# A DiT block on one core: first K block and last x tile loaded by columns, image 0's last K tile spread over the scale bank, other PSUM banks for image 1

## The chip, the cores and the metric

The kernel runs on one core of a Trainium2 chip. The metric is the device time of one execution in microseconds (us); shorter is better. A core has TensorE (PE, the matmuls; PEld are its weight loads), VectorE (DVE), ScalarE (ACT), GpSimd (POOL), SyncE (SP, which issues most loads), an on-chip memory of 128 partitions, and PSUM, eight banks of 512 fp32 columns in which matmuls leave their results and from which DVE and ACT read them.

## The reference

One transformer block with adaptive layer norm: x is 2 images of 256 tokens with D = 1152, in bf16.

```
mod = (silu(c) @ w_mod).reshape(B, 6, 1, D)
shift_a, scale_a, gate_a, shift_m, scale_m, gate_m = [mod[:, i] for i in range(6)]
h = layernorm(x) * (1 + scale_a) + shift_a
q, k, v = split(h @ wqkv), two heads of 576
a = softmax(q k^T * 576**-0.5) v, heads joined, @ wo
x = x + gate_a * a
h2 = layernorm(x) * (1 + scale_m) + shift_m
return x + gate_m * (gelu(h2 @ w_fc1) @ w_fc2)
```

The change lies in the first part: from the loads to the end of k. The shift is left out of k (it adds the same to every score of a query), so k needs only the scaled layer norm, which the kernel calls HK; q and v use HX, which is HK plus the shift.

## The kernel before, in words

D is cut into nine blocks of 128 rows (kt = 0 to 8), the same nine for the contraction and for the output features (f or j = 0 to 8). A token tile t is 128 tokens; tiles 0 and 1 are image 0, tiles 2 and 3 image 1. All loads of the start stand in one SP queue in the order written: x tiles 0 to 2, the scale part of w_mod for kt 0 to 4 (WSC, in four loads), K blocks 0 and 1 (WK), x tile 3, K blocks 2 to 4, WSC for the rest, K blocks 5 to 8, the shift part (WSH), then the Q blocks (WQ, over WSC's place).

PE goes through the start in the order of the program text. Scale matmuls (sca) sum up the scales of blocks 0 to 4 in bank 7, the very first in bank 3. The normalised x (XN) is transposed by tile: xn_T(t) writes nine transposes into the places that xt_ps(b, kt) names. From there hk(kt, b) makes HK = transposed x times scale. For kt 0 to 4 (KC = 5) hk reads PSUM itself (L832 on DVE, L830 on ACT); the others are copied first (xn_T_copy, L688) and scaled once their scales are known. k_pair(kts, i, b) multiplies the K columns of features 2i and 2i+1 with HK of image b, both halves in one bank, KB[b][i]. Image 0 has four pairs in banks 0 to 3. Image 1 has three pairs. What is left over is feature 6 and 7 of image 1 and feature 8 of both images; feature 8 is one projection of 512 columns at the end of the K phase (proj(WK, 8, 17, HK, 7)).

In the middle stands scb: 36 small matmuls that sum up the scales of blocks 5 to 8 in the first 128 columns of bank 7. DVE transposes them in two steps (scb_T5 and scb_T6, L907), adds one (L909), and makes hk_5 to hk_8 from them. After the K pairs come the shift matmuls (sh, bank 0), their transpose on DVE (L952), and HX (L961 on DVE, L958 on ACT). Then q: for each kt six matmuls of 512 columns into six banks:

```
qb = (2, 3, 4, 5, 6, 1)
for kt in range(KT):
    for j in range(KG):
        mm(ps32(qb[j]), WQ[:, kt, j * 128:(j + 1) * 128], HX[:, kt, :], kt == 0, kt == KT - 1)
```

A small planner orders the work and inserts the waits. PE and SP keep the order of the text. ACT and DVE begin with lists written by hand (S.first): DVE has hk_0_1, hk_2_1, hk_4_1, scb_T5, sc1a_5, hk_5_0, hk_5_1, scb_T6, sc1a_6 near the end of its list, ACT ends with xn_2, hk_4_0, hk_1_1, hk_3_1, xnT_cp1_5 (the second number is the image). After its list an engine takes, of what is ready by the planner's own durations, the operation with the longest remaining path. Waits come from what each instruction reads and writes. In PSUM the planner keeps books by whole bank:

```
if eng == "pe":
    if self.bank_other[b]:
        self.bank_prev_other[b] = self.bank_other[b]
        self.bank_other[b] = []
        self.bank_pe[b] = []
    for o in self.bank_prev_other[b]:
        self._add_dep(ins, o)
...
else:
    for u in self.bank_pe[b]:
        self._add_dep(ins, u.instrs[-1])
    for o in self.bank_other[b]:
        if o.unit.eng != eng:
            self._add_dep(ins, o)
```

That is: a matmul that writes a bank waits for all operations of ACT and DVE that read the bank earlier in the text; an operation of ACT or DVE waits for the last matmul of each PE unit in the bank, and for all earlier operations of the other of the two engines in that bank.

Behind the K phase and q follow scores and softmax, v, the output projection, the second layer norm and the MLP; the change doesn't touch them.

Of the kernel before, what the change touches and what calls it, by code (L numbers as in the profile page):

```python
# [497 lines left out]
P = 128  # L498
NTOK = 512
D = 1152  # L500
KT = 9
# [5 lines left out]
CH = 384  # L507
NCH = 3
F0 = 9
KC = 5  # L510
# [5 lines left out]
def c_mm(n):  # L516
    return max(n / 2.4 + 2.5, 27.0)


def c_act(n, aps=0):  # L520
    return 190.0 + 0.8 * n + 75.0 * aps


def c_dve_psum32(n):
    return 110.0 + 1.13 * n


def c_dve_psum16(n):
    return 110.0 + 0.57 * n
# [14 lines left out]
def build_kernel(nc, x, c, wqkv, wo, w_mod, w_fc1, w_fc2, out):  # L544
    S = Sched()
# [4 lines left out]
    with (  # L550
# [4 lines left out]
        def sb(off, nbytes, dt=BF16):  # L555
            assert off % 4 == 0 and off + nbytes <= ARENA_BYTES, (off, nbytes)
            v = arena[:, off // 2:(off + nbytes) // 2]
            if dt == F32:
                v = v.bitcast(F32)
            return v  # L560

        def ps32(bank, c0=0, n=512):
            return psum[:, bank * 512 + c0: bank * 512 + c0 + n]

        def ps16(bank, c0=0, n=1024):
            v = psum[:, bank * 512: (bank + 1) * 512].bitcast(BF16)
            return v[:, c0:c0 + n]
# [21 lines left out]
        def wmat(o, f):  # L589
            return sb(o, KT * f * 2).rearrange("p (k f) -> p k f", k=KT)  # L590
# [3 lines left out]
        WK = wmat(O_B, D)  # L594
# [10 lines left out]
        X = sb(O_X, 9216).rearrange("p (t d) -> p t d", t=4)  # L605
        XN = sb(O_QK, 9216).rearrange("p (t d) -> p t d", t=4)
        HX = sb(O_HX, 9216).rearrange("p (k t) -> p k t", k=KT)
        HK = sb(O_HK, 9216).rearrange("p (k t) -> p k t", k=KT)
        QK = sb(O_QK, 18432).rearrange("p (j t) -> p j t", j=18)
# [54 lines left out]
        xv = x.rearrange("b (p t) d -> b p t d", t=2)  # L664
        outv = out.rearrange("b (p t) d -> b p t d", t=2)
        wqkv_v = wqkv.rearrange("(k p) f -> p k f", p=P)
# [5 lines left out]
        def dma(dst, src, nbytes, name, is_out=False, eng="sp", run=4096):  # L672
            eff = 1.0 if run >= 4096 else (1.08 if run >= 2304 else (1.15 if run >= 1536 else (1.3 if run >= 1024 else 1.42)))
            return S.op(eng, 500.0 if eng == "sp" else 150.0, lambda e: e.dma_start(dst, src), reads=[src], writes=[dst],  # L674
                        name=name, dma_bytes=nbytes * eff, is_out=is_out)

        def dve(cost, fn, reads, writes, name):
            return S.op("dve", cost, fn, reads=reads, writes=writes, name=name)

        def act(cost, fn, reads, writes, name):  # L680
            return S.op("act", cost, fn, reads=reads, writes=writes, name=name)
# [4 lines left out]
        def copy_on(eng, dst, src, n, psum16, name):  # L686
            if eng == "act":
                act(c_act(n), lambda e: e.activation(out=dst, in_=src, func=ACTF.Copy), [src], [dst], name)  # L688
            else:
                dve(c_dve_psum16(n) if psum16 else c_dve_psum32(n), lambda e: e.tensor_copy(dst, src), [src], [dst], name)  # L690

        def mm(o, l, r, st, sp, **kw):
            S.instr(lambda e: e.matmul(o, lhsT=l, rhs=r, start=st, stop=sp, **kw), reads=[l, r], writes=[o])  # L693

        def tr(o, i_, idn):
            S.instr(lambda e: e.transpose(o, i_, idn), reads=[i_, idn], writes=[o])  # L696
# [6 lines left out]
        for (ka, kb, cuts) in ((0, KC, (0, 2, 5, 8, 9)), (KC, KT, (0, 3, 6, 9))):  # L703
            w = (kb - ka) * P
            for k0, k1 in zip(cuts, cuts[1:]):
                dma(WSC[:, k0:k1, ka * P:kb * P], wmod_v[:, k0:k1, D + ka * P:D + kb * P], (k1 - k0) * P * w * 2,
                    "ld_sc%d_%d" % (ka, k0), run=w * 2)
            for kt in range(ka, kb):
                dma(WK[:, kt, :], wqkv_v[:, kt, D:2 * D], P * D * 2, "ld_wk%d" % kt, run=2304)
                if kt == 1:  # L710
                    dma(X[:, 3, :], xv[1][:, 1, :], P * D * 2, "ld_x3", run=2304)
        for k0 in range(0, KT, 3):
            dma(WSH[:, k0:k0 + 3, :], wmod_v[:, k0:k0 + 3, 0:D], 3 * P * D * 2, "ld_sh%d" % k0, run=2304)

# [61 lines left out]

        def xt_ps(b, kt, n=1):
            if b == 0:
                return (4, 5, 6)[kt // 4], (kt % 4) * 256
            return (7, (kt - KC) * 256) if kt >= KC else ((6, 4)[kt % 2], kt // 2 * 256)  # L780

        def xn_T(t, part="", kts=range(KT)):
            b = t // 2
            S.unit("pe", len(kts) * c_mm(128), "xnT_%d%s" % (t, part))
            for kt in kts:
                bank, c0 = xt_ps(b, kt)
                tr(ps16(bank, c0 + (t % 2) * 128, 128), XN[:, t, kt * 128:(kt + 1) * 128], IDENT)
# [47 lines left out]
        def k_mm(kts, j, b, bank, half):  # L835

            for kt in kts:
                mm(ps32(bank, half * 256, 256), WK[:, kt, j * 128:(j + 1) * 128], HK[:, kt, b * 256:(b + 1) * 256], kt == 0 and half == 0,
                   kt == KT - 1, skip_group_check=True)

        KB = [(0, 1, 2, 3), (5, 6, 4)]
        ev_rr = [0]

        def k_pair(kts, i, b, bank=None):
            S.unit("pe", 2 * len(kts) * c_mm(256), "k%d_%d_%d" % (b, i, kts[0]))
            bank = KB[b][i] if bank is None else bank
            if kts[0] == 0:
                for kt in kts:
                    for half in range(2):
                        k_mm((kt,), 2 * i + half, b, bank, half)  # L850
            else:
                for half in range(2):
                    k_mm(kts, 2 * i + half, b, bank, half)
            if kts[-1] == KT - 1:
                eng = "act" if ev_rr[0] % 2 == 0 else "dve"
                ev_rr[0] += 1
                copy_on(eng, QK[:, 9 + 2 * i:11 + 2 * i, b * 256:(b + 1) * 256], ps32(bank).rearrange("p (j t) -> p j t", j=2), 512, False,
                        "k_ev%d_%d" % (b, i))
# [25 lines left out]
        for kt in range(KC):  # L884
            for i in range(2 if kt == KC - 1 else 4):
                k_pair((kt,), i, 0)
            if kt == 1:
                xn_T(2)
        xn_T(3, "a", range(KC))
        k_pair((KC - 1,), 2, 0)  # L890
        xn_T(3, "b", range(KC, KT))
# [3 lines left out]
            hk(kt, 1, "act" if kt % 2 else "dve")  # L895
        k_pair((0, 2, 1, 4, 3), 0, 1)
        k_pair((0, 2, 1), 1, 1)
        S.unit("pe", KC * c_mm(256), "k1_6_0")
        for i, kt in enumerate((0, 2, 1, 4, 3)):
            mm(ps32(7, 256, 256), WK[:, kt, 768:896], HK[:, kt, 256:512], i == 0, False, skip_group_check=True)  # L900
        S.unit("pe", KT * 4 * 27.0, "scb")
        for kt in range(KT):
            quad_mm(7, WSC[:, kt, :], KC, KT, kt, False)
# [8 lines left out]
                hk(kt, b)  # L912
        k_pair((4, 3), 1, 1)
        k_pair((0, 2, 1, 4, 3), 2, 1)
        for kt in range(KT):
            dma(WQ[:, kt, :], wqkv_v[:, kt, 0:D], P * D * 2, "ld_wq%d" % kt, run=2304)
        for kt in range(KC, KT - 2):
# [7 lines left out]
        def qk_evac(j, bank):  # L925
            copy_on("act" if ev_rr[0] % 2 == 0 else "dve", QK[:, j, :], ps32(bank), 512, False, "qk_ev%d" % j)
            ev_rr[0] += 1

        def proj(W, j, dst_j, H, bank):
            S.unit("pe", KT * c_mm(512), "qk_%d" % dst_j)  # L930
            for kt in range(KT):
                mm(ps32(bank), W[:, kt, j * 128:(j + 1) * 128], H[:, kt, :], kt == 0, kt == KT - 1)
            if dst_j == 17:
                qk_evac(dst_j, bank)
            else:
                copy_on("act", QK[:, dst_j, :], ps32(bank), 512, False, "qk_ev%d" % dst_j)

        for f, bank, c0, kts in ((6, 7, 256, range(KC, KT)), (7, 1, 0, range(KT))):
            S.unit("pe", len(kts) * c_mm(256), "k1_%d_%d" % (f, kts[0]))
            for kt in kts:  # L940
                mm(ps32(bank, c0, 256), WK[:, kt, f * 128:(f + 1) * 128], HK[:, kt, 256:512], kt == 0, kt == KT - 1, skip_group_check=f == 6)
            copy_on("act", QK[:, 9 + f, 256:512], ps32(bank, c0, 256), 256, False, "k_ev1_f%d" % f)
        S.unit("pe", KT * 4 * 31.0 + 100.0, "sh")
        for kt in range(KT):
            quad_mm(0, WSH[:, kt, :], 0, 9, kt)
# [7 lines left out]
        for kt in range(KT):  # L953
            for b in range(2):
# [5 lines left out]
                else:  # L960
                    dve(260, lambda e, src=src, dst=dst, s2=s2: e.tensor_scalar(out=dst, in0=src, scalar1=s2, scalar2=None, op0=ALU.add),  # L961
                        [src, s2], [dst], "hx_%d_%d" % (kt, b))
        proj(WK, 8, 17, HK, 7)
        dma(WO, wo_v, D * D * 2, "ld_wo", run=2304)


# [238 lines left out]
        for j, eng in ((5, "act"), (1, "dve"), (2, "act"), (3, "dve"), (4, "act"), (0, "act")):  # L1205
            copy_on(eng, QK[:, j, :], ps32(qb[j]), 512, False, "qk_ev%d" % j)
        proj(WQ, 6, 6, HX, 0)
        proj(WQ, 7, 7, HX, 1)
        s_halves()
        s_and_softmax(0, 0)  # L1210
# [62 lines left out]
        for t in range(4):  # L1273
            b = t // 2
# [69 lines left out]
```

## Time and profile before

| | |
|---|---|
| median of three runs | 243.71 us (243.59 to 245.18) |
| the profiled execution | 243.42 us, its span 241.7 us |
| PE busy | 235.7 us, 98% of the span |
| DVE, ACT busy | 115.9 and 68.0 us |
| granted TensorE clock | 1.000 |
| first matmul of K | 10.91 us after the span's start |
| first matmul of q | 32.06 us |
| DMA, first 70 us | 375 GB/s on average |

The span runs from the first to the last instruction of the program; the execution's time has some 1.7 us more around it. A row of the timeline gives start, length, engine, line of the kernel, operation, output and inputs, number of instructions, and in brackets how long the engine was idle before and what ended that. A matmul's length runs to its modelled end and overlaps the next one; the pace of PE is read from the starts. Where a helper records all operations of a kind (L688 for copies, L693 for matmuls, L696 for transposes), the shape and the order tell which one it is.

### The profile page before, as it was taken

What the parts mean: (1) busy time and instruction counts of PE and PEld (TensorE: products, weight loads), DVE (VectorE), ACT (ScalarE), POOL (GpSimd) and SP (SyncE); (2) the same over time, 40 slices, a digit from 0 to 9 for tenths busy, and PEclk for the clock granted to TensorE, in tenths of its full rate; (3) what the DMA queues carried; (4) which work ended last, traced back from release to release, by engine and by line L of the source; (5) the groups of instructions that cost most, each with busy time, mean ns of one, the idle gap of its engine ahead of it and who ended that gap; (6) DMA issues with size and microseconds to landing.
All of it is one profiled execution on the core that took longest, in us unless ns stands there. A gap on an engine that the chain in (4) does not pass through costs nothing.

```text
span 241.7 us, 3956 instructions
## 1 busy us (share of the span) xinstructions
PE 235.7 (98%) x1691; PEld 144.3 (60%) x1699; DVE 115.9 (48%) x229; ACT 68.0 (28%) x137; POOL 21.4 (9%) x38
## 2 busy tenths in 40 slices
PE   6899999999999999999999999999999999999995
PEld 2688844466657666898544444444556666566664
DVE  2654358888994589669999500000122111111112
ACT  4940540546324126973322222333000000000000
POOL 1300000000021476300000110000000000000000
DMA  6999999999994999999963499000000000000000
GB/s 220 369 374 391 390 387 386 404 414 407 391 356 124 321 379 391 392 355 394 343 209 86 122 342 376 8 0 3 0 16 19 16 16 16 19 19 27 22 17 16
DMA packets 30427, 51.58 MB, mean 213 GB/s; under 512 B 1611, under 2 KB 16971, under 8 KB 30411
## 3 DMA queue, kind: packets, MB, share of 16 engines
q1 hardware_dynamic: 29888, 50.73, 58.8%
q0 software_dynamic: 352, 0.60, 0.8%
q8 instruction: 13, 0.21, 0.4%
q10 hardware_dynamic: 171, 0.01, 0.0%
q14 instruction: 3, 0.02, 0.0%
HBM read 50.15 MB, written 1.19 MB: 212 GB/s over the span
## 4 chain that ended last, share of the span: by engine, by line
PE 94%; DMA 3%; SPq 1%; issue 0%; DVE 0%
PE psum L693 92%; DMA arena<-in_wqkv_dram 3%; PE psum L696 2%; SPq L674 1%; DVE arena L1286 0%; DVE arena L1287 0%
## 5 line engine op out<-in xcount | busy, mean ns | idle before, releaser
L693 PE MATMUL psum<-arena 128*128 128x384 bf16 (+9 forms) x1602 | 232.4, 313 | 2.8 <-POOL arena L719 1.5
L693 PEld LDWEIGHTS psum<-arena 128*128 128x128 bf16 (+2 forms) x1610 | 139.0, 97 | 92.0 <-issue 3.8
L1286 DVE TENSOR_TENSOR arena<-psum,arena 128x384 f32<-128x384 f32 (+2 forms) x13 | 6.9, 528 | 88.5 <-PE psum L693 88.5
L1196 ACT ACTIVATE arena<-psum 128x512 bf16<-128x512 f32 (+1 forms) x45 | 22.8, 511 | 42.2 <-PE psum L693 42.2
L688 ACT ACTIVATE arena<-psum 128x512 bf16<-128x512 f32 (+7 forms) x35 | 18.4, 550 | 37.5 <-PE psum L693 37.5
L1091 DVE SCALAR_TENSOR_TENSOR arena<-arena 128x1152 f32<-128x1152 bf16 x16 | 21.3, 1409 | 0.0
L1062 DVE SCALAR_TENSOR_TENSOR arena<-arena 128x896 f32<-128x896 bf16 x16 | 17.7, 1145 | 0.0
L1162 POOL TENSOR_TENSOR arena<-arena 128x384 f32<-128x384 f32 x12 | 10.9, 912 | 13.3 <-DVE arena L1161 11.1
L674 POOL DMA_DIRECT2D dit_scratch<-arena x6 | 3.6, 603 | 92.6 <-ACT arena L688 53.1
L741 DVE BATCH_NORM_STATS2 arena<-arena 128x6 f32<-128x384 f32 (+1 forms) x18 | 9.5, 550 | 4.0 <-DMA arena<-in_x_dram 3.9
L690 DVE CAST arena<-psum 128x512 bf16<-128x512 f32 x11 | 7.5, 690 | 7.4 <-PE psum L693 7.4
L1161 DVE TENSOR_TENSOR arena<-psum,arena 128x384 f32<-128x384 f32 x12 | 6.7, 555 | 3.8 <-PE psum L693 3.8
L1167 ACT ACTIVATE arena<-arena 128x1152 bf16<-128x1152 f32 x4 | 5.4, 1344 | 9.8 <-DVE arena L1166 9.8
L696 PE MATMUL psum<-arena 128*128 128x128 bf16 (+1 forms) x89 | 7.1, 219 | 0.4 <-DMA arena<-in_c_dram 0.4
L696 PEld LDWEIGHTS psum<-arena 128*128 128x128 bf16 (+1 forms) x89 | 5.8, 98 | 2.4 <-DMA arena<-in_c_dram 1.3
L1287 DVE TENSOR_TENSOR arena<-arena 128x384 bf16<-128x384 f32 (+2 forms) x13 | 6.9, 528 | 0.5
L1186 ACT ACTIVATE arena<-psum,arena 128x128 bf16<-128x128 bf16 x16 | 6.1, 455 | 3.0 <-PE psum L696 2.2
L1183 DVE TENSOR_SCALAR arena<-psum,arena 128x128 bf16<-128x128 bf16 x20 | 5.5, 336 | 2.9 <-PE psum L696 2.9
L1005 ACT ACTIVATE arena<-psum,arena 128x256 bf16<-128x256 f32 x8 | 3.7, 469 | 0.4 <-DVE arena L1002 0.3
L745 POOL TENSOR_TENSOR arena<-arena 128x1 f32<-128x1 f32 x6 | 3.3, 553 | 4.5 <-DVE arena L744 4.3
L1001 DVE TENSOR_REDUCE arena<-psum 128x2 f32<-128x512 f32 x4 | 2.7, 686 | 0.9 <-PE psum L693 0.9
L1059 DVE TENSOR_SCALAR arena<-arena 128x896 f32<-128x896 bf16 x2 | 1.3, 684 | 3.6 <-DMA arena<-in_w_mod_dram 3.6
(60 smaller groups left out, 54.1 us busy)
## 6 DMA issues: line engine op xcount, KB each, us to landing
arena<-in_w_fc_dram SPq DMA_DIRECT2D x9, 1152.0 KB, 8.1
arena<-in_w_fc_dram SPq DMA_DIRECT2D x4, 2592.0 KB, 17.5
arena<-in_w_mod_dram SPq DMA_DIRECT2D x3, 1920.0 KB, 19.7
arena<-in_wqkv_dram SPq DMA_DIRECT2D x18, 288.0 KB, 10.0
arena<-in_w_mod_dram SPq DMA_DIRECT2D x3, 864.0 KB, 12.6
arena<-in_wqkv_dram SPq DMA_DIRECT2D x1, 2592.0 KB, 16.9
arena<-in_wo_dram SPq DMA_DIRECT2D x1, 2592.0 KB, 26.1
arena<-in_w_mod_dram SPq DMA_DIRECT2D x1, 2592.0 KB, 18.2
```

The costliest lines, as they stand in the source:

```text
L688: act(c_act(n), lambda e: e.activation(out=dst, in_=src, func=ACTF.Copy), [src], [dst], name)
L690: dve(c_dve_psum16(n) if psum16 else c_dve_psum32(n), lambda e: e.tensor_copy(dst, src), [src], [dst], name)
L693: S.instr(lambda e: e.matmul(o, lhsT=l, rhs=r, start=st, stop=sp, **kw), reads=[l, r], writes=[o])
L696: S.instr(lambda e: e.transpose(o, i_, idn), reads=[i_, idn], writes=[o])
L741: dve(550, lambda e, s=s, o=o: e.bn_stats(out=o, in_=s), [s], [o], "bn_%s_%d" % (tag, ci))
L1062: dve(150 + FG * 1.1, lambda e, o=o, w=w, s1=s1: e.scalar_tensor_tensor(out=o, in0=w, scalar=s1, in1=o, op0=ALU.mult, op1=ALU.add), [w, s1 ...
L1091: u = dve(1300, lambda e, o=o, w=w, s1=s1: e.scalar_tensor_tensor(out=o, in0=w, scalar=s1, in1=o, op0=ALU.mult, op1=ALU.add), [w, s1, o], ...
L1161: dve(550, lambda e, o=o, ga=ga, x1c=x1c: e.tensor_tensor(out=x1c, in0=o, in1=ga, op=ALU.mult), [o, ga], [x1c], "wo_t1_%d_%d" % (t, ci))
L1162: S.op("pool", 930, lambda e, xs=xs, x1c=x1c: e.tensor_tensor(out=x1c, in0=x1c, in1=xs, op=ALU.add), reads=[x1c, xs], writes=[x1c], name=" ...
L1196: act(c_act(ntok), lambda e: e.activation(out=dst, in_=o, func=ACTF.Gelu_apprx_tanh), [o], [dst], "gelu_%d_%d" % (f, tok0))
L1286: dve(c_dve_psum32(w), lambda e, o=o, gm=gm, t1=t1: e.tensor_tensor(out=t1, in0=o, in1=gm, op=ALU.mult), [o, gm], [t1], "fc2_t1_%d_%d" % ( ...
L1287: dve(c_dve_32(w), lambda e, t1=t1, x1c=x1c, ost=ost: e.tensor_tensor(out=ost, in0=t1, in1=x1c, op=ALU.add), [t1, x1c], [ost], "fc2_out_%d ...
```

## The change

It has four parts.

- K block 0 is loaded in two DMAs, columns 0 to 511 and 512 to 1151; x tile 3 in two, columns 0 to 383 and 384 to 1151.
- The transposes lie in other places. For image 0, tile kt = 4 goes to bank 6 (columns from 768, in 16-bit elements), beside kt = 8; the rest stays in banks 4 and 5. For image 1, kt 0 to 3 go to bank 4, kt 4 to bank 6, kt 5 to 8 to bank 5; before, they were in banks 6 and 4 in turn, and in bank 7. The pairs of image 1 go to banks 6, 4, 5 (before: 5, 6, 4).
- Feature 8 of image 0 is summed up in the free half of bank 7 in three places (k_8): kt 0 and 1 after xn_T(2), kt 2 to 4 after scb and two more pairs, kt 5 to 8 near the end. Feature 6 of image 1, which stood in that half, is summed up in one piece in bank 1; feature 7 in bank 2; feature 8 of image 1 by itself in bank 3, just ahead of q.
- A pair that begins with kt = 0 now runs all its kt for one half, then for the other.

```diff
             for kt in range(ka, kb):
-                dma(WK[:, kt, :], wqkv_v[:, kt, D:2 * D], P * D * 2, "ld_wk%d" % kt, run=2304)
+                for c0, c1 in ((0, 512), (512, D)) if kt == 0 else ((0, D),):
+                    dma(WK[:, kt, c0:c1], wqkv_v[:, kt, D + c0:D + c1], P * (c1 - c0) * 2, "ld_wk%d_%d" % (kt, c0), run=(c1 - c0) * 2)
                 if kt == 1:
-                    dma(X[:, 3, :], xv[1][:, 1, :], P * D * 2, "ld_x3", run=2304)
+                    for c0, c1 in ((0, CH), (CH, D)):
+                        dma(X[:, 3, c0:c1], xv[1][:, 1, c0:c1], P * (c1 - c0) * 2, "ld_x3_%d" % c0, run=(c1 - c0) * 2)
...
         def xt_ps(b, kt, n=1):
             if b == 0:
-                return (4, 5, 6)[kt // 4], (kt % 4) * 256
-            return (7, (kt - KC) * 256) if kt >= KC else ((6, 4)[kt % 2], kt // 2 * 256)
+                return (6, 768) if kt == KC - 1 else ((4, 5, 6)[kt // 4], (kt % 4) * 256)
+            return (5, (kt - KC) * 256) if kt >= KC else (6, 512) if kt == KC - 1 else (4, kt * 256)
...
-        KB = [(0, 1, 2, 3), (5, 6, 4)]
+        KB = [(0, 1, 2, 3), (6, 4, 5)]
         ev_rr = [0]
+
+        def k_8(kts):
+            S.unit("pe", len(kts) * c_mm(256), "k0_8_%d" % kts[0])
+            for kt in kts:
+                mm(ps32(7, 256, 256), WK[:, kt, 1024:D], HK[:, kt, 0:256], kt == 0, kt == KT - 1, skip_group_check=True)
+            if kts[-1] == KT - 1:
+                copy_on("act", QK[:, 17, 0:256], ps32(7, 256, 256), 256, False, "k_ev0_f8")
 
         def k_pair(kts, i, b, bank=None):
...
-            if kts[0] == 0:
-                for kt in kts:
-                    for half in range(2):
-                        k_mm((kt,), 2 * i + half, b, bank, half)
-            else:
-                for half in range(2):
-                    k_mm(kts, 2 * i + half, b, bank, half)
+            for half in range(2):
+                k_mm(kts, 2 * i + half, b, bank, half)
...
             if kt == 1:
                 xn_T(2)
+                k_8((0, 1))
...
         k_pair((0, 2, 1, 4, 3), 0, 1)
         k_pair((0, 2, 1), 1, 1)
-        S.unit("pe", KC * c_mm(256), "k1_6_0")
-        for i, kt in enumerate((0, 2, 1, 4, 3)):
-            mm(ps32(7, 256, 256), WK[:, kt, 768:896], HK[:, kt, 256:512], i == 0, False, skip_group_check=True)
         S.unit("pe", KT * 4 * 27.0, "scb")
...
         k_pair((4, 3), 1, 1)
         k_pair((0, 2, 1, 4, 3), 2, 1)
+        k_8((2, 3, 4))
...
-            if dst_j == 17:
-                qk_evac(dst_j, bank)
-            else:
-                copy_on("act", QK[:, dst_j, :], ps32(bank), 512, False, "qk_ev%d" % dst_j)
-
-        for f, bank, c0, kts in ((6, 7, 256, range(KC, KT)), (7, 1, 0, range(KT))):
-            S.unit("pe", len(kts) * c_mm(256), "k1_%d_%d" % (f, kts[0]))
-            for kt in kts:
-                mm(ps32(bank, c0, 256), WK[:, kt, f * 128:(f + 1) * 128], HK[:, kt, 256:512], kt == 0, kt == KT - 1, skip_group_check=f == 6)
-            copy_on("act", QK[:, 9 + f, 256:512], ps32(bank, c0, 256), 256, False, "k_ev1_f%d" % f)
+            copy_on("act", QK[:, dst_j, :], ps32(bank), 512, False, "qk_ev%d" % dst_j)
+
+        def k1_tile(f, bank):
+            S.unit("pe", KT * c_mm(256), "k1_%d" % f)
+            for kt in range(KT):
+                mm(ps32(bank, 0, 256), WK[:, kt, f * 128:(f + 1) * 128], HK[:, kt, 256:512], kt == 0, kt == KT - 1)
+            copy_on("act", QK[:, 9 + f, 256:512], ps32(bank, 0, 256), 256, False, "k_ev1_f%d" % f)
+
+        k1_tile(6, 1)
         S.unit("pe", KT * 4 * 31.0 + 100.0, "sh")
...
-        proj(WK, 8, 17, HK, 7)
+        k1_tile(7, 2)
+        k_8(range(KC, KT))
+        k1_tile(8, 3)
         dma(WO, wo_v, D * D * 2, "ld_wo", run=2304)
```

## The prediction

> **What bounds the kernel now.** I read the shares first, then the chain of work that ended last, then the timeline of the stretch that the change touches, in narrow windows.
>
> ```profile
> span 241.7 us, 3956 instructions
> ...
> PE 235.7 (98%) x1691; PEld 144.3 (60%) x1699; DVE 115.9 (48%) x229; ACT 68.0 (28%) x137; POOL 21.4 (9%) x38
> ...
> PE 94%; DMA 3%; SPq 1%; issue 0%; DVE 0%
> ```
>
> ```profile
> 3.79 7.07 DMA arena<-in_wqkv_dram
> ...
> 10.91 1.92 PE psum L693 x16
> ...
> 16.35 13.61 PE psum L693 x178
> ```
>
> The end is set by the DMA of K block 0 (issued 3.79, landed 10.86) and from 10.91 on by PE alone. So a wait of PE is worth its full length and work on another engine is worth nothing, unless it makes PE wait. Rates from the starts of neighbouring matmuls: 0.109 us for 256 columns, 0.056 for a transpose, 0.216 for 512 columns; the first matmul after a wait takes 0.01 more.
>
> The rows of the stretch:
>
> ```profile
> 10.33 0.29 DVE L832 TENSOR_SCALAR arena<-arena,psum 128x256 bf16<-128x256 bf16 x1
> ...
> 12.35 1.48 DVE L741 BATCH_NORM_STATS2 arena<-arena 128x6 f32<-128x384 bf16 x3 [0.40 <-DMA arena<-in_x_dram]
> 12.40 0.45 ACT L830 ACTIVATE arena<-psum,arena 128x256 bf16<-128x256 bf16 x1
> ...
> 15.45 0.28 PEld L696 LDWEIGHTS psum<-arena 128*128 128x128 bf16 x5 [0.22 <-DVE arena L772]
> ...
> 15.95 0.84 ACT L830 ACTIVATE arena<-psum,arena 128x256 bf16<-128x256 bf16 x2 [3.10 <-PE psum L696]
> 15.95 0.87 DVE L832 TENSOR_SCALAR arena<-psum,arena 128x256 bf16<-128x256 bf16 x3 [0.23 <-PE psum L696]
> ...
> 20.25 0.22 DVE L907 STREAM_TRANSPOSE arena<-psum 128x32 f32<-128x32 f32 x1 [3.43 <-PE psum L693]
> ...
> 21.04 7.43 PEld L693 LDWEIGHTS psum<-arena 128*128 128x128 bf16 x69 [0.22 <-DVE arena L832]
> 21.10 0.28 DVE L907 STREAM_TRANSPOSE arena<-psum 128x96 f32<-128x96 f32 x1
> ...
> 28.79 0.38 ACT L688 ACTIVATE arena<-psum 128x256 bf16<-128x256 f32 x1 [0.55 <-PE psum L693]
> ...
> 30.72 2.50 ACT L958 ACTIVATE arena<-arena 128x256 bf16<-128x256 bf16 x6 [1.55 <-DVE arena L952]
> ```
>
> PE waits twice after 10.91: at 15.46 for xn_3a (its start comes 0.215 after the one before, of which 0.11 is wait) and at 21.05 for hk_5_0 (again 0.11). At 15.95 the five hk of image 1 run on ACT and DVE side by side. That they can is a matter of banks, as two later tiles show. In tile 0 ACT and DVE convert out of two banks and start together:
>
> ```profile
> 92.59 1.15 ACT L1186 ACTIVATE arena<-psum,arena 128x128 bf16<-128x128 bf16 x3 [1.94 <-PE psum L696]
> ```
>
> ```profile
> 92.59 0.60 DVE L1183 TENSOR_SCALAR arena<-psum,arena 128x128 bf16<-128x128 bf16 x2
> ```
>
> In tile 3 two of DVE's tiles lie in ACT's bank, and ACT starts 0.10 after DVE's second has ended (105.96), though PE was done 0.7 earlier:
>
> ```profile
> 105.36 0.60 DVE L1183 TENSOR_SCALAR arena<-psum,arena 128x128 bf16<-128x128 bf16 x2 [1.85 <-PE psum L696]
> ```
>
> ```profile
> 106.06 1.16 ACT L1186 ACTIVATE arena<-psum,arena 128x128 bf16<-128x128 bf16 x3 [0.81 <-PE psum L693]
> ```
>
> So the planner's rule (one bank, two engines: a wait, whatever the columns) is a real wait in the trace.
>
> **The change, part by part.**
>
> *K block 0 in two loads.* The first pairs need columns 0 to 511, 128 of 288 KB. The load ahead of it (160 KB, rows of 1280 B) landed at 10.07, 0.46 after the one ahead of that; block 0 came 0.79 later. By bytes the first piece lands near 10.43. The first matmul then waits for hk_0_0 (10.33 + 0.29, and 0.06 to PE): 10.68 instead of 10.91, **-0.23**. The second piece (10.9) is needed at 11.1. But block 1 landed at 11.59 and PE, earlier now, wants it at 11.55. Shorter rows cost something: 160 KB in 0.46 is 0.06 slower for 288 KB than 0.79. Bounds: nothing to 0.13 (two pieces of 0.46); I take 0.06, so 11.65, PE at 11.70: **+0.16** given back, with the restart. SP issues two DMAs more, 0.48 each; these loads are issued 7 to 8 us ahead of landing, so the queue in front of them hides it. The Trainium skill (DMA: Bandwidth & Descriptors, Specifications) has rows of 512 B and more at line rate; by that the 0.06 would be nothing. The 1280 B rows here moved 356 GB/s against about 400 for 2304 B, so the measurement decides.
>
> *x tile 3 in two loads.* BN statistics begin at about 11.95, when DVE is free, not 12.35; xn_3a follows 0.36 earlier. The wait at 15.46 goes: **-0.11**. Two early matmuls of k_8 ahead of it would have covered it too.
>
> *Banks of the transposes.* (a) Image 0's tile 4 now sits in bank 6, where image 1's tile 4 goes. xn_T(2) must therefore wait for hk_4_0 (ACT, 12.40 to 12.85, at PE 12.91); PE is there at 12.81: **+0.11**. (b) Image 1's tiles 0 to 3 share bank 4, read by DVE (hk_0, hk_2) and ACT (hk_1, hk_3): now a chain. (c) k1_0 writes bank 6, which hk_4_1 reads; hk_4_1 stands third on DVE behind hk_2_1. Before, k1_0 had bank 5, which nobody held. PE's order: kt 4 done, xn_T(3a) at 15.60 (two matmuls of k_8 are new), its last result at 16.06, xn_T(3b) and two pairs to 16.54. DVE: hk_0_1 16.08 to 16.43; ACT hk_1_1, after a hand-over of 0.10, 16.53 to 17.00 (0.47); DVE hk_2_1 17.04 to 17.38; hk_4_1, pipelined 0.08 ahead, to 17.64; PE at 17.70. Wait: **+1.17** with the restart. Lower end: without the chain, the three DVE operations take 0.87 and PE waits 0.45. Upper end: both hand-overs to DVE at 0.10, 1.3. The row of tile 3 is nearest, so I take 1.17. What PE wants next (hk_3_1, now at 17.9) is needed at 18.15. The pairs by halves instead of by tiles cost nothing here, since after that wait all tiles are ready.
>
> *k_8 in three places.* Five matmuls move ahead of the pairs of kt 5; five of k1_6 stood there before, so the work is equal. But k_8((2,3,4)) writes bank 7, whose scales scb_T6 (L907, the second) still reads. Before, nothing wrote bank 7 until much later. From the first scb matmul (18.79) to scb_T6's end (21.38) and PE (21.43) are 2.64; PE's work between, scb 0.61 and 14 matmuls 1.54, takes 2.15. Wait **+0.50**; behind it hk_5_0 is long ready, so the old wait at 21.05 goes, **-0.11**. Lower end for the pair: -0.11, if the write needn't wait; upper +0.45.
>
> *Tail of the K phase.* Nine matmuls of 512 columns (1.94) become 18 of 256 (1.97): **+0.02**. DVE loses a cast of 0.69 and ACT gains two copies of 0.38, off the path. The last tile, k1_8, goes to bank 3 and is followed at once by q_kt0, whose second matmul writes bank 3; before, that tile was in bank 7, which q does not use. A copy starts 0.31 after the last matmul's start (28.48 to 28.79), takes 0.38, then 0.06 to PE: 0.75, of which 0.33 is covered by that matmul and q's first. Wait 0.42 if ACT is free. It has the six hx of L958 (0.40 each) and k_ev1_f7; following the planner's priorities, three more hx stand ahead of the copy and end about 0.05 after it could start: **+0.48**. Ends: 0.42, and 0.9 with one hx more in front.
>
> Sum: -0.23 + 0.16 - 0.11 + 0.11 + 1.17 + 0.50 - 0.11 + 0.02 + 0.48 = **+1.99**. PE is on the chain to the end, so nothing behind absorbs it; later loads run ahead of PE or wait for PE and shift with it. The profiled execution, 243.42 us (span 241.7), becomes 245.4; the shown median, 243.71, stands 0.29 above it, so I predict **245.7**. Own range of this case: 1.2 to 2.5 more, 244.9 to 246.2. One per cent (2.4 us) is about what a measurement tells here, since the three runs spread by 1.6.
>
> **Rivals.**
>
> *Half the price.* The hand-overs between ACT and DVE are hidden (or k_8 meets scb_T6 late), only one of the big waits stands: sum about +1.2, 244.9. For it: waits in the trace are often 0.1. Against it: tile 3's row. 12%.
>
> *Not slower.* None of the bank waits reaches PE, for instance because PE arrives later than I reckon everywhere. Then -0.23 + 0.16 - 0.11 - 0.11 + 0.02 = -0.27: 243.4. It decides if PE reaches k1_0 only after 17.7; by the rows it is there at 16.54. 6%.
>
> *ACT in the tail.* The copy of k1_8 stands behind all five hx: they end at about 30.72 + 2.5 + 0.3 in old times, the wait grows by 0.4 to 0.8, q_kt0 stands still: 246.3. For it: the planner's time for an hx and the real one differ (0.47 planned, 0.40 in the row). 12%, slower by over 1%.
>
> *The clock falls.* At the start the rate is half (0.427 between 512-column starts from 1.49 to about 5.2). If a wait of 1.2 us brought that state back for as long, 3.7 us, half would be lost: +1.85 more, 247.5. Against: gaps of 0.4 near 8 us left the rate at 0.109, and the granted clock is 1.00 in each window I asked for, from 10.9 to 44. The Trainium skill (TensorE: Matmul & The Clock Gate, HAM oscillation) puts the fall at idle gaps over about 3.4 us; by that rule it doesn't happen, and no run here shows such a gap. 5%.
>
> **How the numbers follow.** Forecast 62%, half 12%, not slower 6%, ACT 12%, clock 5%, others 3%. Slower by over 1% (above 246.15): the ACT and clock cases and the top of my own range, 0.24. Faster by over 1%: nothing reaches it, 0.02. Within: 0.74. The range leaves out not-slower and the clock: 244.4 to 246.8.
>
> **What would show it.** First matmul of K at 10.7, kt 1 at 11.7; PE idle before k1_0 by 1.1 to 1.2, released by DVE L832, with ACT's and DVE's hk taking turns; a wait of 0.5 on DVE L907 before k_8((2,3,4)); a wait of 0.4 to 0.5 on ACT L688 in q_kt0; no wait on L772. I am wrong if ACT and DVE run hk of image 1 side by side, or if PE has no gap over 0.3 between 10.7 and 36.

## The result and the profile after

The changed kernel takes 245.13 us (median of 8 runs, 244.90 to 245.63), against 243.51 us for the kernel before on the same chip (8 runs). The ratio of the runs is 1.0062, with a 95% interval from 1.0041 to 1.0084: 1.5 us slower (1.0 to 2.0). The profiled execution took 245.19 us, 1.77 more than that of before.

The page of the changed kernel, its shares and its chain:

```profile
span 243.5 us, 3984 instructions
...
PE 236.5 (97%) x1708; PEld 145.1 (60%) x1708; DVE 115.6 (48%) x228; ACT 68.7 (28%) x139; POOL 21.4 (9%) x38
...
PE 92%; DMA 3%; DVE 1%; ACT 1%; SPq 1%; issue 0%
```

PE's share of the chain is 2 points lower, and DVE and ACT now have a share of 1% each. Where they entered stands in the chain of the changed kernel in order of time (start, length, what):

```profile
10.51 0.28 DVE arena L834
...
10.93 1.98 PE psum L693 x16
...
16.62 0.48 ACT arena L832
17.13 0.62 DVE arena L834 x2
...
17.80 3.31 PE psum L693 x58
21.11 0.22 DVE arena L909
...
22.04 0.20 DVE arena L909
...
22.29 9.06 PE psum L693 x105
31.35 0.48 DVE arena L954
...
32.63 1.19 ACT arena L960 x3
33.83 0.28 ACT arena L688
...
34.15 25.97 PE psum L693 x147
```

Before, one piece of PE ran from 16.35 to 29.96. Now the chain leaves PE three times: at 16.62 for an hk on ACT and two on DVE (L832 and L834 are the lines that were L830 and L832), at 21.11 for the scales (L909, before L907; the second transposition, at 22.04, is what PE waits for), and at 31.35 for the shift's transposition on DVE (L954), then hx (L960) and copies on ACT, the last of them the copy of k1_8 (L688) ahead of 34.15. K no longer starts on the landing of block 0 but on hk_0_0 (10.51).

The same stretches in the timeline of the changed kernel (start, busy time, engine, operation, and in brackets the idle time before it with its releaser):

```profile
12.01 1.54 DVE L743 BATCH_NORM_STATS2 arena<-arena 128x6 f32<-128x384 bf16 x3
...
16.18 0.35 DVE L834 TENSOR_SCALAR arena<-psum,arena 128x256 bf16<-128x256 bf16 x1 [0.74 <-PE psum L696]
...
16.62 0.47 ACT L832 ACTIVATE arena<-psum,arena 128x256 bf16<-128x256 bf16 x1 [3.67 <-PE psum L696]
17.13 0.61 DVE L834 TENSOR_SCALAR arena<-psum,arena 128x256 bf16<-128x256 bf16 x2 [0.60 <-ACT arena L832]
17.52 0.47 ACT L832 ACTIVATE arena<-psum,arena 128x256 bf16<-128x256 bf16 x1 [0.42 <-DVE arena L834]
...
17.80 4.16 PE L693 MATMUL psum<-arena 128*128 128x256 bf16 x66 [1.00 <-DVE arena L834]
...
32.53 1.29 ACT L960 ACTIVATE arena<-arena 128x256 bf16<-128x256 bf16 x3
...
33.73 0.36 ACT L688 ACTIVATE arena<-psum 128x256 bf16<-128x256 f32 x1
```

Before, ACT and DVE began image 1's hk together at 15.95. Here DVE does one, ACT one, DVE two, ACT one, each after the other, and PE's next matmul is released by DVE at 17.80. The three hx (L960) end at 33.82 by their row, and the copy of k1_8 stands behind them. The statistics of x tile 3 (12.01) follow on DVE without a wait for a DMA (before: 0.40).

The ends of matmuls are modelled and run on, so the brackets show less than the whole wait. By the starts of neighbouring matmuls, less the usual 0.109 us of a 256-column matmul, PE waited 1.16 us ahead of k1_0, 0.49 ahead of the matmul at 22.29 and 0.495 at q's second matmul. From there to its last matmul PE ran a constant 2.10 us behind the execution of before.

### The profile page after: what moved, and what is told of

Read it like the earlier page. It is cut to its first block, busy times and chain, and to the rows that moved or that the text cites. A ratio compares the mean times of both kernels' runs of the same rounds, so it can differ in the third digit from the quotient of the medians.

```text
span 243.5 us, 3984 instructions
## 1 busy us (share of the span) xinstructions
PE 236.5 (97%) x1708; PEld 145.1 (60%) x1708; DVE 115.6 (48%) x228; ACT 68.7 (28%) x139; POOL 21.4 (9%) x38
## 4 chain that ended last, share of the span: by engine, by line
PE 92%; DMA 3%; DVE 1%; ACT 1%; SPq 1%; issue 0%
PE psum L693 91%; DMA arena<-in_w_mod_dram 3%; PE psum L696 2%; SPq L674 1%; ACT arena L960 1%; DVE arena L834 1%; ACT arena L688 0%; DVE arena L954 0%; ACT arena L832 0%; DVE arena L909 0%; DVE arena L1290 0%; DVE arena L1291 0%; DVE arena L911 0%; DVE arena L822 0%
## 5 line engine op out<-in xcount | busy, mean ns | idle before, releaser
L688 ACT ACTIVATE arena<-psum 128x512 bf16<-128x512 f32 (+7 forms) x37 | 19.2, 540 | 38.0 <-PE psum L693 38.0
L690 DVE CAST arena<-psum 128x512 bf16<-128x512 f32 x10 | 6.8, 691 | 8.8 <-PE psum L693 8.8
L960 ACT ACTIVATE arena<-arena 128x256 bf16<-128x256 bf16 x6 | 2.7, 498 | 1.5 <-DVE arena L954 1.5
```

## The experiments

The four theories to tell apart: the three waits cost what the traces show, one by one (mine); the wait before k1_0 is one thing, not a chain of turns and a write after a read; the two loads gain nothing; or they gain something that the waits in the profiles don't show.

**Another bank for k1_8** (bank 0, which nobody holds by then; from the changed kernel):

```diff
-        k1_tile(8, 3)
+        k1_tile(8, 0)
```

> The changed kernel, but with the last K tile (feature 8 of image 1) in bank 0 instead of bank 3. Theory (PE waits at q's second matmul only because its bank still holds that tile): the wait of 0.50 us released by ACT's copy goes and nothing takes its place; everything before is unchanged, the first q matmuls follow each other at 0.216, and the time is 0.5 us below the changed kernel, about 244.6, 1.004 to 1.005 of the kernel before. Rival (q is late because HX is late, ACT having more to do): a wait of about the same length stays, released by an hx of ACT or DVE, and the time is that of the changed kernel, 1.006 to 1.007.

Measured: 244.67 us, ratio to the kernel before 1.0046 (1.0031 to 1.0061). The timeline of this kernel around q's start:

```profile
31.74 3.53 PE L693 MATMUL psum<-arena 128*128 128x256 bf16 x22
...
34.46 0.63 ACT L688 ACTIVATE arena<-psum 128x256 bf16<-128x256 f32 x2
```

ACT's copies are now as late as 34.46 and PE doesn't mind: q's first matmuls of 512 columns come 0.216 apart. The other two waits stayed (1.16 ahead of 17.73, 0.50 ahead of 22.23). So the third wait is the bank of k1_8 alone.

**Three matmuls of k_8 back behind the scales** (from the changed kernel):

```diff
-        k_8((2, 3, 4))
...
-        k_8(range(KC, KT))
+        k_8(range(2, KT))
```

> The changed kernel, but with image 0's feature 8, kt 2 to 4, done at the end together with kt 5 to 8, not between the scale matmuls and the pairs of kt 5. Theory (those three matmuls wait for DVE's second transposition out of the same bank): the wait of 0.49 released by that transposition goes; PE has three matmuls less to cover the scales' way and waits 0.11 for hk_5_0 again, as in the kernel before; net 0.38 less than the changed kernel, about 244.7. Rival (the scales themselves come late in the changed kernel): PE waits 0.4 or more for hk_5_0 and the time stays.

Measured: 244.75 us, ratio 1.0048 (1.0031 to 1.0065). The timeline of this kernel where the wait was:

```profile
21.78 0.48 DVE L834 TENSOR_SCALAR arena<-arena 128x256 bf16<-128x256 bf16 x2
22.12 0.66 PEld L693 LDWEIGHTS psum<-arena 128*128 128x128 bf16 x7 [0.23 <-DVE arena L834]
```

The wait of 0.49 for L909 is gone and the old one of 0.11 for hk_5_0 (L834) is back. The 1.16 ahead of k1_0 remained.

**Image 1 in alternating banks, image 0 as before** (from the changed kernel; image 1's tiles 5 to 8 stay in bank 5):

```diff
-                return (6, 768) if kt == KC - 1 else ((4, 5, 6)[kt // 4], (kt % 4) * 256)
-            return (5, (kt - KC) * 256) if kt >= KC else (6, 512) if kt == KC - 1 else (4, kt * 256)
+                return (4, 5, 6)[kt // 4], (kt % 4) * 256
+            return (5, (kt - KC) * 256) if kt >= KC else ((6, 4)[kt % 2], kt // 2 * 256)
```

> The changed kernel, but with image 0's tile 4 back in bank 5 and image 1's tiles 0 to 4 back in banks 6 and 4 in turn, so that DVE and ACT read different banks; the pairs of image 1 stay in 6, 4, 5. Theory (two causes in one wait: the turn-taking of ACT and DVE over bank 4, and the first pair's bank 6 being read by DVE): the five hk run side by side again, PE still waits for the third of DVE, but 0.45 to 0.5 instead of 1.16; 0.7 less, about 244.4. Rival A (the reuse of bank 6 alone): the wait stays near 1.16 and the time as it was. Rival B (the turn-taking alone): no wait is left, 1.2 less, about 243.9.

Measured: 244.80 us, ratio 1.0054 (1.0039 to 1.0069). The timeline of this kernel:

```profile
16.16 0.87 DVE L834 TENSOR_SCALAR arena<-psum,arena 128x256 bf16<-128x256 bf16 x3 [0.66 <-PE psum L696]
16.16 0.84 ACT L832 ACTIVATE arena<-psum,arena 128x256 bf16<-128x256 bf16 x2 [3.23 <-PE psum L696]
...
17.09 0.72 PE L693 MATMUL psum<-arena 128*128 128x256 bf16 x5 [0.30 <-DVE arena L834]
```

ACT and DVE start together again, and k1_0 starts at 17.09 instead of 17.80. The wait that is left is 0.47: k1_0 still writes bank 6, which DVE reads until 17.03. In the profile the turns cost 0.7 us. The time missed the expected 244.4 by 0.4: the ratio fell by only 0.0008 against the changed kernel where 0.003 would be 0.7 us. Both intervals are about 0.0015 to 0.002 wide on each side, so the timing doesn't show the 0.7 by itself.

**Only the turns, in the kernel before** (image 1's tiles 0 to 3 all in bank 4; the first pair of image 1 stays in bank 5, which nobody reads):

```diff
-            return (7, (kt - KC) * 256) if kt >= KC else ((6, 4)[kt % 2], kt // 2 * 256)
+            return (7, (kt - KC) * 256) if kt >= KC else (6, 512) if kt == KC - 1 else (4, kt * 256)
```

> The kernel before, with image 1's tiles 0 to 3 in bank 4 and tile 4 in bank 6 (as in the changed kernel) and nothing else changed: the first pair of image 1 still has bank 5, which nobody reads. Theory (the turn-taking of ACT and DVE over one bank costs PE time by itself): the hk of tiles 0, 1, 2, 3 run one after another; that pair starts on time with tile 0, then waits for hk_2_1 by 0.65 to 0.7; time 0.7 more than before, 244.3, ratio 1.003. Rival (only the reuse of bank 6 made PE wait): ACT and DVE overlap or PE is not held; ratio 1.000.

Measured: 244.21 us against 243.65, ratio 1.0025 (1.0014 to 1.0036): 0.6 us (0.3 to 0.9). The timeline of this kernel:

```profile
16.53 0.35 DVE L832 TENSOR_SCALAR arena<-psum,arena 128x256 bf16<-128x256 bf16 x1 [0.23 <-PE psum L696]
...
16.98 0.47 ACT L830 ACTIVATE arena<-psum,arena 128x256 bf16<-128x256 bf16 x1 [4.03 <-PE psum L696]
17.49 0.61 DVE L832 TENSOR_SCALAR arena<-psum,arena 128x256 bf16<-128x256 bf16 x2 [0.60 <-ACT arena L830]
...
17.90 0.61 PE L693 MATMUL psum<-arena 128*128 128x256 bf16 x4 [0.52 <-DVE arena L832]
```

The turns are there, and this time PE waits for hk_2_1 itself, its operand: 0.685 by the starts. With the 0.47 of the run above that makes 1.15, against 1.16 in the changed kernel. So the long wait has two causes that add: four reads of one bank by two engines in turn, and a write of PE to a bank that is still being read.

**All three edits together** (bank 0 for k1_8, k_8 late, alternating banks):

> The changed kernel with the three edits together: last K tile in bank 0, kt 2 to 4 of feature 8 at the end, image 1's tiles in banks 6 and 4 in turn. Theory (each wait is on PE's path by itself and they add up): 0.5 + 0.38 + 0.7 = 1.6 less than the changed kernel, PE at its first q matmul 0.5 us later than in the kernel before, what is left being the wait for bank 6; about 244.0, 1.002 of the kernel before. Rival (the waits cover for one another or for the loads, which come 0.15 later): less than 1.2 regained, 1.003 or more.

Measured: 243.72 us, ratio 1.0008 (0.9998 to 1.0017). Of the waits only the 0.47 ahead of k1_0 is left, and yet the time is nearly that of before. The profiled execution was the slowest of its ten (244.34): the last scale load of its group landed at 20.09, the latest of all executions here, and block 1 at 12.08 (11.74 in the changed kernel). Its timeline shows PE waiting for the former:

```profile
20.14 2.08 PE L693 MATMUL psum<-arena 128*2 128x128 bf16 x27 [0.38 <-DMA arena<-in_w_mod_dram]
```

That wait belongs to the landing of this execution. With a wait of 0.47 left, a ratio of 1.002 was due if the two loads gave nothing. That it is lower raised the next question.

**The loads alone, in the kernel before.** First x tile 3 in two loads:

```diff
-                    dma(X[:, 3, :], xv[1][:, 1, :], P * D * 2, "ld_x3", run=2304)
+                    for c0, c1 in ((0, CH), (CH, D)):
+                        dma(X[:, 3, c0:c1], xv[1][:, 1, c0:c1], P * (c1 - c0) * 2, "ld_x3_%d" % c0, run=(c1 - c0) * 2)
```

> The kernel before, with x tile 3 in two loads and nothing else changed. Theory (the only thing it can buy is PE's wait of 0.11 for xn_3a, and the scale loads, which land 0.4 before PE needs the last of them, let that through): xn_3a 0.3 earlier, no wait of PE on it, 0.1 less than before, 243.4, ratio 0.9996. Rival (the scales' way binds): PE is at the scale matmuls 0.1 earlier and waits 0.1 longer for hk_5_0; ratio 1.000.

Measured: 243.61 against 243.62, ratio 0.9996 (0.9982 to 1.0011). The wait for xn_3a is gone from the profile; its 0.11 us is too small for this timing.

Then K block 0 in two loads:

```diff
-                dma(WK[:, kt, :], wqkv_v[:, kt, D:2 * D], P * D * 2, "ld_wk%d" % kt, run=2304)
+                for c0, c1 in ((0, 512), (512, D)) if kt == 0 else ((0, D),):
+                    dma(WK[:, kt, c0:c1], wqkv_v[:, kt, D + c0:D + c1], P * (c1 - c0) * 2, "ld_wk%d_%d" % (kt, c0), run=(c1 - c0) * 2)
```

> The kernel before, with K block 0 in two loads and nothing else changed. Theory (the first matmul of K gains at most 0.1, because hk_0_0 is ready only 0.05 to 0.1 before block 0 lands, and kt 1 then waits for block 1, which lands 0.03 to 0.2 later than with one load): kt 1 starts no earlier than before, counted from the landing of the last scale load ahead of block 0 (1.72 us behind it in the profile before); time the same or up to 0.1 more, ratio 1.000 to 1.0005. Rival, the sum of the prediction (0.23 at the first matmul, 0.16 of it given back): kt 1 starts 0.08 earlier, ratio 0.9997.

Measured: 243.62 against 243.62, ratio 0.9993 (0.9980 to 1.0006). In the profile the first K matmul starts at 10.87 and kt 1, which waits for block 1, at 11.86: 1.76 after the landing of the scale load ahead of block 0, where it was 1.72 before. One execution shows no gain, and the time can't tell.

Then both:

> The kernel before, with both loads in two pieces and nothing else changed. Theory: the two effects add, 0.1 gained at xn_3a and nothing or a small loss at block 1; 243.4 to 243.6, ratio 0.9995 to 1.0003. Rival (the early loads are the change's real gain and the bank waits hide it): 0.25 less, ratio 0.9990.

Measured: 243.27 against 243.62, ratio 0.9986 (0.9972 to 1.0000): about 0.3 us gained, with nothing at the edge of the interval. The two single loads gained 0.01 and 0.00 by the medians, so this isn't their sum. A second execution was profiled for the landings alone:

> The same kernel as the one with both loads in two pieces, for a second profile: the first was taken in an execution in which the TensorE clock was at half rate from 7.9 to 11.1 us after a wait of 1.13 us. Theory (that fall belongs to the execution and its late first scale load, not to the kernel): granted clock 1.00 throughout, first matmul of K at 10.7 to 10.9, no wait for xn_3a, span about 241.4. Rival (the kernel brings the clock down): half rate again before 12 us.

It took 243.45 us. The clock stayed at 1.00 and PE didn't wait for xn_3a, as expected; the times were missed. The span was 241.7, the first K matmul came at 11.09, since the scale load ahead landed at 10.31, and kt 1 at 12.15 after waiting 0.19 for block 1. Across the executions that load landed between 9.85 and 10.52 and block 1 between 11.59 and 12.20, whichever the kernel. So one profile can't weigh a gain of 0.2 us in the loads.

What the twelve traces do show is where the 0.3 us lies: at the end of the program. From the start of the last matmul to the landing of the last store it is 2.19 to 2.21 us in every kernel. From that landing to the end of the span it is not the same:

| loads in two pieces | profiled executions | last landing to the end |
|---|---|---|
| none or one | before, the turns, x tile 3 alone, block 0 alone | 0.80, 0.80, 0.81, 0.83 us |
| both | the other eight | 0.49 to 0.50 us |

In the four kernels of the first row SP stands for 0.39 to 0.41 us at one point between its last wait and the end; in the eight others none of its pauses there is over 0.15. With both loads split SP issues two DMAs more than before; why that takes the pause away no run here shows. So both splits together are worth 0.31 us at the end, which is nearly all of the 0.34 by the ratio, and an earlier start of K isn't shown to be worth anything. In the kernel with the three edits 0.47 less 0.31 is 0.16, and 0.19 was measured (-0.05 to 0.41).

**Filling the hole** (alternating banks and bank 0 as above, and the three matmuls of k_8 moved ahead of the first pair of image 1, where PE had to wait for hk_4_1):

```diff
+        k_8((2, 3, 4))
         k_pair((0, 2, 1, 4, 3), 0, 1)
...
         k_pair((0, 2, 1, 4, 3), 2, 1)
-        k_8((2, 3, 4))
```

> The changed kernel with the last K tile in bank 0, image 1's tiles in banks 6 and 4 in turn, and kt 2 to 4 of image 0's feature 8 put ahead of the first pair of image 1, into the hole where PE waits for bank 6. Theory (these three matmuls wait for nothing there): the wait ahead of that pair falls from 0.47 to 0.14, the wait for the scales' transposition does not come back, and hk_5_0 is waited for by 0.1; 0.33 less than the kernel with all three edits, about 243.4, ratio 0.9995. Rival (the late scale loads hold PE there anyway): what is gained ahead of the pair is waited for at the scale matmuls; 243.7, ratio 1.0008.

Measured: 243.45 us against 243.62, ratio 0.9987 (0.9975 to 0.9999). The timeline of this kernel:

```profile
16.11 0.87 DVE L834 TENSOR_SCALAR arena<-psum,arena 128x256 bf16<-128x256 bf16 x3 [0.66 <-PE psum L696]
...
16.35 1.41 PE L693 MATMUL psum<-arena 128*128 128x256 bf16 x10
...
17.03 0.55 PEld L693 LDWEIGHTS psum<-arena 128*128 128x128 bf16 x6 [0.25 <-DVE arena L834]
```

PE now has three matmuls to do while DVE works, and waits 0.14 at 17.04 instead of 0.47. They write bank 7 ahead of the scales, so the wait for L909 is gone too. The 0.1 expected at hk_5_0 didn't come; PE waited 0.15 for a scale load instead (landed 19.29). By the ratio this version is 0.3 us faster than the kernel before, by the medians 0.17, and the interval only just leaves out no change. In the profiles the gain against before is the program's end (0.50 us here): PE's last matmul starts at 238.78, before's at 238.67. Against the changed kernel the median is 1.7 us lower.

## Why the prediction was right

The forecast was 245.7 us (244.4 to 246.8) and a change of less than 1%; 245.13 us was measured, 0.6% above before. The three large waits came as described, with their releasers and their lengths, so I go through the terms of the sum. In the profiled execution they make +0.08 (kt 1 at 11.876, before 11.792) + 0.04 - 0.11 + 1.17 + 0.50 - 0.11 + 0.02 + 0.50 = +2.09, and the trace shows PE 2.10 behind; the sum said 1.99.

- *k1_0's wait*: 1.17 forecast, 1.17 with its restart. The choice of the chain over the lower end of 0.45 rested on the rows of a later tile, and those carried over: 0.68 for the turns and 0.47 for the bank were shown apart.
- *k_8 and the scales*: 0.50 forecast, 0.50 with its restart, with the old wait of 0.11 gone. Most of the way to the scales isn't work of DVE: the 36 small matmuls start within 0.46 us, but DVE's first transposition starts 1.45 us after the first of them (19.65 to 21.10), since their completions come 0.034 us apart in the trace.
- *q and the copy of k1_8*: 0.48 forecast, 0.50. Three hx stood ahead of the copy, as worked out; the rival with five didn't come.
- *xn_T(2) and hk_4_0*: 0.11 forecast, 0.04. PE came there later, which covers most of it.
- *xn_3a*: -0.11, as forecast.
- *K's start*: this term of the sum was off. -0.23 and +0.16 were forecast; here the first K matmul came at 10.93 (forecast 10.68, before 10.91) and kt 1 at 11.88 (forecast 11.70), 0.08 later than before. Three steps were wrong. I let hk_0_0 start at 10.33, as in the execution of before, but it also needs the copy of the transposed tile (L690, below), which here ended 0.18 later because the second scale load landed at 8.44 and not at 8.22 and held up the transposes. I gave 0.06 to the hand-over to PE, which took 0.14: hk_0_0 ended at 10.79, and PE's wait there needs an instruction of its own for the second semaphore (10.83 to 10.88 in the trace). And kt 1 waits for block 1, which landed at 11.74 (forecast 11.65), with the same 0.14 behind it. The step treated one execution's landings as the kernel's.

The copy in the kernel before, then the copy and hk_0_0 in the changed one:

```profile
9.92 0.28 DVE L690 COPY arena<-psum 128x256 bf16<-128x256 bf16 x1
...
10.10 0.29 DVE L690 COPY arena<-psum 128x256 bf16<-128x256 bf16 x1
...
10.49 0.29 DVE L834 TENSOR_SCALAR arena<-arena,psum 128x256 bf16<-128x256 bf16 x1
```

In the kernel with bank 0 for k1_8 the last scale load landed at 10.10, nearly as early as in before (10.07), and hk_0_0 still started at 10.49, 0.11 behind the same copy.

The 0.06 for shorter rows isn't borne out either. By the rows it was taken from it is 0.04 (0.46 x 288 / 160 = 0.83, against 0.79), and the 0.46 was one landing: in the other executions that load came 0.39 to 0.60 behind the one ahead. The two pieces of block 0 together took 0.76 to 0.94 in nine executions, the block in one load 0.76 to 0.93 in three.

One term was put at nothing without being looked at: the end of the program, which came 0.31 us shorter (0.80 to 0.49) with both loads split. "PE is on the chain to the end, so nothing behind absorbs it" holds up to PE's last matmul, 2.10 behind, but not for what SP does after the last store. 2.10 - 0.31 = 1.79, and the two profiled executions differ by 1.77. In the timing 1.62 was measured by the medians and 1.5 (1.0 to 2.0) by the ratio. The sums of the other kernels fit in the same way, each inside its interval: 1.28 us with k1_8 in bank 0 (measured 1.1, 0.8 to 1.5), 1.39 with k_8 late (1.2, 0.8 to 1.6), 1.1 with alternating banks (1.3, 0.9 to 1.7). So the forecast lies 0.57 too high mainly for two reasons: this end, and a start from the median of three runs (243.71, where eight gave 243.51). The error at K's start went the other way, so a part of the closeness is luck; the three waits aren't.

A record is missing in the trace of before, the first matmul of feature 8's projection: it was due at 29.89, and the next comes 0.444 after the one before it. Counting without it puts q's first matmul at 32.06, as in the table of before; it started at 31.84. No difference in the sum above uses it.

Of the rivals, half the price and not slower fall with the 1.17 and 0.50. The clock stayed at 1.00 through the 1.16 us wait.

What stays open: why the split of both loads shortens the end, whether either split starts K earlier on average, and the price of the turns in the changed kernel by timing alone (0.7 us in its profile; 0.6 timed in the kernel before).

## What to carry to other kernels

Where PE is the chain to the end, write down for each PSUM bank who reads it, in which order on which engine, and when PE writes it next: three changes of place that left the work as it was each became a wait here, and their prices could be read from rows of before. Where waits are kept by whole bank, as here, a free half of a bank isn't free while the other half is read. A wait that can't be removed can be filled with matmuls into a bank nobody holds, which won back most of two waits here. And when the time doesn't follow the waits, compare what lies behind the last matmul too: 0.3 us that looked like a gain of early loads lay there.

## What was new in the hardware

**The clock fell after a wait of 1.13 us, in one profiled execution.** In the profiled execution of the kernel with both loads split (244.61 us) the first scale load landed at 7.47 and PE stood from 6.4 to 7.5. Its busy time by windows (PEclk is the granted clock, the third number from the end):

```profile
7.00:9.00 2.00, 1.48 (x13) 0.69 (x14) 1.27 (x4) 1.97 (x5) 1.15 (x2) 0.68 1.03 365
9.00:10.00 1.00, 1.00 (x19) 0.70 (x18) 0.30 (x3) 0.60 (x2) 0.00 (x0) 0.50 1.08 388
10.00:11.00 1.00, 1.00 (x13) 1.00 (x11) 0.00 (x0) 0.00 (x0) 0.55 (x1) 0.50 1.05 384
...
12.00:13.00 1.00, 0.64 (x11) 0.52 (x9) 0.92 (x6) 1.00 (x3) 0.00 (x0) 1.00 1.05 386
```

The granted clock was 0.50 from about 7.7 to 11.1 us, transposes came 0.107 apart instead of 0.056, K's first matmul was at 12.52, and the span was 242.8 us where the other profiled execution of the same kernel had 241.7 with the clock at 1.00. (The granted clock shows only such a fall: it reads 1.00 at the start too, where 512-column matmuls came 0.427 apart.) It doesn't take this kernel: three of the 35 executions of before in the same set have the same mean granted clock, 0.993, and took 245.08 to 245.32 us. In the changed kernel an idle time of 0.71 at the same place left the clock at 1.00, and so did 1.16 between dense matmuls. The Trainium skill (TensorE: Matmul & The Clock Gate, HAM oscillation — how this bites in real kernels) puts the fall at PE idle gaps over about 3.4 us; this execution fell after a third of that, so the trace doesn't agree, and the measurement decides. That the one wait brought the clock down isn't shown either: in the 3.41 us from the clock's rise at 4.32 to its fall at 7.74 PE was busy for 1.96, and in the same length after the rise for 2.68 in the changed kernel and 2.54 with block 0 alone split, where the clock stayed up. What decides it no run here shows.

**The landing of one load varies by 0.6 to 0.7 us from execution to execution.** The scale load ahead of block 0 landed between 9.85 and 10.52 with the same loads ahead of it in all twelve executions, and block 1, where block 0 is one load, at 11.59, 12.14 and 12.20. With a PE that waits for each block as it comes, that scatter is larger than the gain that a split load was to bring.
